# A six-layer cross network on one core: the first half's remainder columns as one load behind the second group, put in order by VectorE, and a first layer without its add

## The chip, the cores and the metric

The kernel runs on one core of one Trainium2 chip. The metric is the device time in microseconds (us) of one execution, as the median of several. The kernel before took 130.63 us (three runs, 130.57 to 130.87). One further execution was recorded by the profiler; it took 130.73 us, and its profile covers a span of 128.9 us. All durations below come from that execution.

## What is computed

The input x0 has 4096 rows of 416 bf16 numbers. Six weight matrices of 416 x 416 and six bias rows are given. Each layer multiplies x0, element by element, with an affine function of the running x, and adds x:

```python
def reference(x0, ws, bs):
    x = x0
    for l in range(ws.shape[0]):
        x = x0 * (x @ ws[l] + bs[l]) + x
    return x
```

In the first layer x is x0 itself, so there the formula is x0 * (x0 @ w + b + 1).

## The kernel before

**Layout.** The work is done transposed: features lie on partitions, rows of x0 along the free axis. The 416 columns are cut into three blocks of 128 (the main blocks, `m` or `k` = 0, 1, 2) and a remainder of 32. The 4096 rows are cut into two halves (`s` = 0, 1) of four groups (`g` = 0 to 3) of 512 rows. `XM[i]` holds the main blocks of x (`XM[0]` those of x0, for good). `XR[i]` holds the remainder: its four bands of 32 partitions are the four groups of a half. `XRd` is a copy of `XR[0]` with its upper and lower 64 partitions exchanged.

**How x0 comes in.** Each group of 512 rows comes by one transposing DMA (`load_x0t`, L75), eight in all, issued on SyncE's queue (SP) in the order (0,0), (0,1), (0,2), (0,3), (1,0) to (1,3). They are called transposed loads here. The 32 remainder columns come as plain row segments of 64 bytes and are transposed by TensorE:

- first half: four loads of 32 KB on ScalarE's queue (`load_xrem0`, L80), each straight into the column order that the transposes want (`xrig[:, 0]`);
- second half: one load of 128 KB on SP's queue (`load_xrem1`, L84) between the transposed loads (1,0) and (1,1), into `xrem`; GpSimd then puts it into column order (L132).

`x0_rem` (L155 to L158) makes four 128x128 transposes into PSUM, and VectorE copies the result three times: to `XR[0]` and, in two halves, to `XRd`. The remainder rows of the first layer's weights (`load_wr0`, L87) come on SP's queue between the transposed loads (0,1) and (0,2), and are spread to the other three bands by ScalarE (L108) and GpSimd (L110). A DMA takes one of eight semaphores in turn, and a DMA whose semaphore was used before waits, on its queue, for that earlier DMA to land.

**The first layer** (`first_layer`, once for each half). TensorE's order in the first half is: the three main blocks of group 0 (`full`, L212, nine matmuls), the four transposes of `x0_rem`, the three main blocks of group 1 (nine matmuls), eight small matmuls with the remainder (`row`, L219), then block 0 of group 2 and of group 3, block 1 of both, block 2 of both, four more `row` matmuls, the remainder's own output (`mm_rem`, L191 and L196), and the second half's four transposes. The second half goes the same way, but takes block by block both groups. ScalarE takes every result out of PSUM with the bias added (`ew_main` L163, `ew_rem` L171), VectorE multiplies by x0 (L164, L172) and adds x (L167, L173).

**After that** come layers 1 to 4, which keep the data in place and are fed by the same three steps (TensorE L179 and L185, ScalarE L163, VectorE L164 and L167), and a last layer that computes untransposed output rows (L325 to L334, ScalarE L352, VectorE L353 and L342) and sends them out.

PSUM has four slots of two banks. Within an engine, instructions run in the order in which they stand; a scheduler may move them unless `tc.keep_in_program_order` pins them.

Of the kernel before, what the change touches and what calls it, by code (L numbers as in the profile page):

```python
# [10 lines left out]
ALU = mybir.AluOpType  # L11
BF16 = mybir.dt.bfloat16
# [4 lines left out]
def kernel(  # L17
# [7 lines left out]
    nc = tc.nc  # L25
    B, D = x0.shape
    L = ws.shape[0]
    P = 128
    NK = 3
    R = D - NK * P  # L30
    assert R == 32 and B == 4096 and D == 416 and L >= 2
    NS = 2
    NG = 4
    CW = 512
# [5 lines left out]
    big = ctx.enter_context(tc.tile_pool(name="big", bufs=1))  # L40
# [4 lines left out]
    x0_v = x0.rearrange("(bt p) d -> p bt d", p=P)  # L45
    out_v = out.rearrange("(bt p) d -> p bt d", p=P)

    ident = const.tile([P, P], BF16)
# [3 lines left out]
    WR = const.tile([P, L, D], BF16)  # L52
# [3 lines left out]
    bM = const.tile([P, NK, L], FP32)  # L56
    bR = const.tile([P, L], FP32)
    X0rows = big.tile([P, NBT, D], BF16)
    XLrows = big.tile([P, NBT, D], BF16)
    scrR = [big.tile([P, 4, P], BF16, name=f"scrR{s}") for s in range(NS)]  # L60
    xrem = big.tile([P, 16, R], BF16)
    xrig = big.tile([P, NS, 4, P], BF16)
    XRd = big.tile([P, NS * CW], BF16)
    XM = [big.tile([P, NK, B], BF16, name=f"XM{i}") for i in range(3)]
    XR = [big.tile([P, NS * CW], BF16, name=f"XR{i}") for i in range(3)]

    def col0(s, g):
        return SW * s + CW * g

    def load_wm(eng, l):  # L70
        eng.dma_start(WM[:, l], ws[l, 0:NK * P, :].rearrange("(k p) n -> p k n", p=P))

    def load_x0t(s, g):
        c0 = col0(s, g)
        nc.sync.dma_start_transpose(out=XM[0][:, :, c0:c0 + CW], in_=x0[c0:c0 + CW, 0:NK * P])  # L75

    def load_xrem0():
        with nc.allow_non_contiguous_dma(reason="64B row segments"):
            for i in range(4):
                nc.scalar.dma_start(xrig[:, 0, i, :].rearrange("p (g r) -> p g r", g=NG), x0_v[:, i:16:4, NK * P:D])  # L80

    def load_xrem1():
        with nc.allow_non_contiguous_dma(reason="64B row segments"):
            nc.sync.dma_start(xrem[:], x0_v[:, 16:32, NK * P:D])  # L84

    def load_wr0():
        nc.sync.dma_start(WR[0:R, 0, :], ws[0, NK * P:D, :])  # L87

    def load_wr(eng, g, l0, l1):
        eng.dma_start(WR[32 * g:32 * g + 32, l0:l1, :], ws[l0:l1, NK * P:D, :].rearrange("l r n -> r l n"))  # L90
# [7 lines left out]
    load_x0t(0, 0)  # L98
    load_wm(nc.scalar, 0)
    nc.scalar.dma_start(bsb[:], bs[:, :])  # L100
    load_x0t(0, 1)
    load_xrem0()
    load_wr0()
    nc.scalar.activation(dz[:, 1:2], dz[:, 0:1], ACT.Identity, bias=dz[:, 0:1], scale=1.0)  # L104
    for g in range(1, NG):
        dst, src = WR[32 * g:32 * g + 32, 0, :], WR[0:R, 0, :]
# [4 lines left out]
    for g in range(2, NG):  # L111
        load_x0t(0, g)
    load_x0t(1, 0)
    load_xrem1()
    for g in range(1, NG):
        load_x0t(1, g)
    load_wm(nc.sync, 1)
# [9 lines left out]
    def fill_wd(l0, l1):  # L127
        for g in range(NG):
            nc.gpsimd.tensor_copy(WD[32 * g:32 * g + 32, l0:l1, g, :], WR[32 * g:32 * g + 32, l0:l1, NK * P:D])  # L129

    fill_wd(0, 1)
    nc.gpsimd.tensor_copy(xrig[:, 1].rearrange("p i (g r) -> p i g r", g=NG), xrem[:].rearrange("p (g i) r -> p i g r", g=NG))  # L132
    fill_wd(1, L)

    wps = psum.tile([P, CW], FP32, tag="ps", name="wps")
# [8 lines left out]
    def bias_setup():  # L144
        pb = psum.tile([P, 4, 8], BF16, tag="ps", name="pb")
        for m in range(NK):
            nc.tensor.transpose(pb[:, m, 0:L], bsb[0:L, 128 * m:128 * m + 128], ident[0:L, 0:L])
        for g in range(NG):
            nc.tensor.transpose(pb[32 * g:32 * g + 32, 3, 0:L], bsb[0:L, NK * P:D], ident[0:L, 0:L], tile_position=(0, 32 * g))
        nc.vector.tensor_copy(bM[:], pb[:, 0:NK, 0:L])  # L150
        nc.vector.tensor_copy(bR[:], pb[:, 3, 0:L])

    def x0_rem(s, tpr):
        for i in range(4):
            nc.tensor.transpose(tpr[:, 128 * i:128 * i + 128], xrig[:, s, i, :], ident[:])  # L155
        for dst, src in ((slice(0, P), slice(0, P)), (slice(64, P), slice(0, 64)), (slice(0, 64), slice(64, P))):
            to = XR[0] if dst == src else XRd
            nc.vector.tensor_copy(to[dst, CW * s:CW * s + CW], tpr[src])  # L158

    def ew_main(l, s, m, h, pt, cur, nxt, pin=False):  # L160
        c0 = col0(s, 2 * h)
        t = tpool.tile([P, 2 * CW], BF16, name="t")
        nc.scalar.activation(t[:], pt[:].rearrange("p a b -> p (a b)"), ACT.Identity, bias=bM[:, m, l:l + 1], scale=1.0)  # L163
        prod = nc.vector.tensor_tensor(out=t[:], in0=t[:], in1=XM[0][:, m, c0:c0 + 2 * CW], op=ALU.mult)  # L164
        if pin:
            tc.keep_in_program_order(prod)
        nc.vector.tensor_tensor(out=nxt[:, m, c0:c0 + 2 * CW], in0=t[:], in1=cur[:, m, c0:c0 + 2 * CW], op=ALU.add)  # L167

    def ew_rem(l, s, pr, curR, nxtR):
        tr = tpool.tile([P, 2 * CW], BF16, name="t")  # L170
        nc.scalar.activation(tr[:, 0:CW], pr, ACT.Identity, bias=bR[:, l:l + 1], scale=1.0)  # L171
        nc.vector.tensor_tensor(out=tr[:, 0:CW], in0=tr[:, 0:CW], in1=XR[0][:, CW * s:CW * s + CW], op=ALU.mult)  # L172
        nc.vector.tensor_tensor(out=nxtR[:, CW * s:CW * s + CW], in0=tr[:, 0:CW], in1=curR[:, CW * s:CW * s + CW], op=ALU.add)  # L173

    def mm_full(l, s, m, g, pts, cur, first, last):
        c0 = col0(s, g)
# [12 lines left out]
    def mm_rem(l, s, pr, cur, curR):  # L189
        for g in range(NG):  # L190
            nc.tensor.matmul(pr[32 * g:32 * g + 32, :], lhsT=WD[:, l, g, :], rhs=curR[:, CW * s:CW * s + CW],  # L191
                             start=True, stop=False, tile_position=(0, 32 * g))
        for k in range(NK):
            for g in range(NG):
                c0 = col0(s, g)
                nc.tensor.matmul(pr[32 * g:32 * g + 32, :], lhsT=WM[:, l, k, NK * P:D], rhs=cur[:, k, c0:c0 + CW],  # L196
                      start=False, stop=(k == NK - 1), tile_position=(0, 32 * g))
# [8 lines left out]
    def first_layer(s):  # L206
        cur, curR, nxt, nxtR = XM[0], XR[0], XM[1], XR[1]

        def full(pt, m, h, gl, after_row):
            c0 = col0(s, 2 * h + gl)  # L210
            for k in range(NK):
                nc.tensor.matmul(pt[:, gl, :], lhsT=WM[:, 0, k, 128 * m:128 * m + 128], rhs=cur[:, k, c0:c0 + CW],  # L212
                                 start=(k == 0 and not after_row), stop=(k == NK - 1 and after_row))

        def row(pt, m, h, opens):
            for gl in range(2):
                rg = 32 * ((2 * h + gl) ^ (2 if m == 1 else 0))
                src = XRd if m == 1 else curR
                nc.tensor.matmul(pt[:, gl, :], lhsT=WR[rg:rg + 32, 0, 128 * m:128 * m + 128],  # L219
                                 rhs=src[rg:rg + 32, CW * s:CW * s + CW],  # L220
                                 start=opens, stop=not opens, tile_position=(rg, 0))

        def ph(m):
            return psum.tile([P, 2, CW], FP32, tag="ps", name=f"ph{m}")

        pa = [ph(m) for m in range(NK)]
        if s == 0:
            for m in range(NK):
                full(pa[m], m, 0, 0, False)
            tp0 = psum.tile([P, CW], BF16, tag="ps", name="tpr")  # L230
            x0_rem(0, tp0[:])
            for m in range(NK):
                full(pa[m], m, 0, 1, False)
        else:
            for m in range(NK):
                for gl in range(2):
                    full(pa[m], m, 0, gl, False)
        pb = [ph(0)]
        row(pa[0], 0, 0, False)
        row(pb[0], 0, 1, True)  # L240
        row(pa[2], 2, 0, False)
        row(pa[1], 1, 0, False)
        for m in range(NK):
            ew_main(0, s, m, 0, pa[m], cur, nxt)
        for m in range(NK):
            if m:
                pb.append(ph(m))
            for gl in range(2):
                full(pb[m], m, 1, gl, m == 0)
        row(pb[1], 1, 1, False)  # L250
        row(pb[2], 2, 1, False)
        pr = psum.tile([P, 2, CW], FP32, tag="ps", name="pr")
        mm_rem(0, s, pr[:, 0, :], cur, curR)
        if s == 0:
            x0_rem(1, pr[:, 1, :].bitcast(BF16)[:, 0:CW])
        for m in range(NK):
            ew_main(0, s, m, 1, pb[m], cur, nxt, pin=(s == 0))
        ew_rem(0, s, pr[:, 0, :], curR, nxtR)

    bias_setup()  # L260
    pe_filler(1, CW)
    for s in range(NS):
        first_layer(s)
# [15 lines left out]
    cur, curR = XM[1], XR[1]  # L279
    for l in range(1, LL):  # L280
        nxt, nxtR = XM[1 + (l % 2)], XR[1 + (l % 2)]
# [29 lines left out]
        cur, curR = nxt, nxtR  # L311

    l = LL
# [97 lines left out]
```

## Time and profile before

| what | value |
|---|---|
| median of three runs | 130.63 us |
| the profiled execution, its time / its span | 130.73 / 128.9 us |
| TensorE (PE) busy | 122.8 us, 95% of the span |
| VectorE (DVE) busy | 106.7 us, 83% |
| ScalarE (ACT) busy | 86.9 us, 67% |
| GpSimd (POOL) busy | 6.3 us, 5% |
| granted TensorE clock, mean | 0.99 |
| share of the chain that ended last | PE 80%, DMA 8%, DVE 5% |
| DVE t<-t,XM L164 and XM<-t,XM L167, 128x1024 | 60 of each, 690 and 697 ns |
| DVE L172 and L173, 128x512 | 10 of each, 419 and 424 ns |
| DVE copies in `x0_rem` L158 | 425 ns (XR), 422 ns (each half of XRd) |
| POOL copy into column order L132 | 665 ns |

The chain that ended last is followed back from the last instruction: at each step to what released it, or to the instruction before it on its engine. Busy shares are averages over stages, so what an edit is worth has to be read in its own stage. A DMA row names the queue that issues it: SPq for SyncE's, ACTq for ScalarE's; its duration is that of the issue, not of the transfer, whose end is called its landing.

### The profile page before, as it was taken

How to read it: one execution, taken by the hardware profiler on the slowest of the kernel's cores; microseconds unless marked ns; L12 is line 12 of the kernel's file. 1: busy time of each engine (PE TensorE's matmuls, PEld its weight loads, DVE VectorE, ACT ScalarE, POOL GpSimd, SP SyncE). 2: the span in 40 equal slices, each digit the busy share in tenths (PEclk: the TensorE clock that was granted, in tenths of full speed). 3: DMA queues.
4: the chain of work that ended last, by engine and by line, in shares of the span. 5: the costliest groups of instructions: out<-in, count | busy, mean ns of one | idle time of the engine just before them, and what ended most of it. 6: DMA issues, size and time to landing. Idle time of an engine off the chain costs nothing.

```text
span 128.9 us, 3971 instructions
## 1 busy us (share of the span) xinstructions
PE 122.8 (95%) x1689; PEld 55.0 (43%) x1691; DVE 106.7 (83%) x195; ACT 86.9 (67%) x99; POOL 6.3 (5%) x18
## 2 busy tenths in 40 slices
PE   7899999999999999999999999999999999999960
PEld 3333343344444454444344444444444345445430
DVE  0032979999999898989898989898989899898991
ACT  0426783987849577848667848668848896569670
POOL 4022200620000000000000000000000000000000
PEclk9999999999999999999999999999999999999996
DMA  3999999999990000000000000000297999995754
GB/s 93 248 200 218 166 164 241 235 330 333 335 324 16 5 0 8 0 0 5 0 5 0 5 0 5 0 5 0 40 167 164 123 226 176 195 311 186 230 179 141
DMA packets 42102, 16.37 MB, mean 127 GB/s; under 512 B 30906, under 2 KB 42084, under 8 KB 42084
## 3 DMA queue, kind: packets, MB, share of 16 engines
q1 hardware_dynamic: 39416, 15.56, 54.4%
q10 hardware_dynamic: 2668, 0.56, 2.4%
q8 instruction: 13, 0.21, 0.7%
q14 instruction: 5, 0.04, 0.1%
HBM read 6.15 MB, written 3.41 MB: 74 GB/s over the span
## 4 chain that ended last, share of the span: by engine, by line
PE 80%; DMA 8%; DVE 5%; issue 2%; SPq 1%; ACT 1%; DVEq 0%
PE pt L179 49%; PE ph L212 9%; DMA XM<-in_x_dram 8%; PE py L325 8%; PE pt L185 5%; PE pr L196 5%; DVE t L353 3%; DVE o L342 2%; PE pr L191 2%; SPq L75 1%; PE py L331 1%; PE ph L219 1%; PE py L334 1%; ACT t L352 1%; PE pr L155 0%
## 5 line engine op out<-in xcount | busy, mean ns | idle before, releaser
L179 PE MATMUL pt<-XM,WM 128*32 128x512 bf16 x1152 | 65.2, 379 | 0.0
L163 ACT ACTIVATE t<-pt,bM 128x1024 bf16<-128x1024 f32 x48 | 49.6, 1115 | 18.3 <-PE pt L185 18.3
L164 DVE TENSOR_TENSOR t<-t,XM 128x1024 bf16<-128x1024 bf16 x60 | 41.4, 690 | 5.3 <-ACT t L163 5.3
L167 DVE TENSOR_TENSOR XM<-t,XM 128x1024 bf16<-128x1024 bf16 x60 | 41.8, 697 | 3.4
L179 PEld LDWEIGHTS <-WM 128*32 128x32 bf16 x1152 | 29.7, 97 | 33.8 <-issue 5.1
L352 ACT CAST t<-py 128x416 bf16<-128x416 f32 (+1 forms) x23 | 14.8, 642 | 4.8 <-PE py L325 2.1
L325 PE MATMUL py<-WM,XM 128*128 128x416 bf16 x96 | 17.7, 340 | 0.0
L212 PE MATMUL ph<-XM,WM 128*128 128x512 bf16 x70 | 16.4, 379 | 0.8 <-DMA XM<-in_x_dram 0.7
L163 ACT ACTIVATE t<-ph,bM 128x1024 bf16<-128x1024 f32 x12 | 12.5, 1113 | 4.4 <-PE ph L219 4.4
L325 PEld LDWEIGHTS <-XM 128*128 128x128 bf16 x96 | 9.0, 98 | 8.5 <-issue 1.4
L353 DVE TENSOR_TENSOR t<-t,X0rows 128x416 bf16<-128x416 bf16 (+1 forms) x23 | 10.4, 455 | 1.2 <-ACT t L352 1.2
L212 PEld LDWEIGHTS <-WM 128*128 128x128 bf16 x72 | 6.8, 97 | 9.1 <-issue 1.8
L342 DVE TENSOR_TENSOR o<-t,XLrows 128x416 bf16<-128x416 bf16 (+1 forms) x23 | 10.3, 453 | 0.0
L171 ACT ACTIVATE t<-pr,bR 128x512 bf16<-128x512 f32 x10 | 6.4, 685 | 2.7 <-PE pr L196 2.1
L196 PE MATMUL pr<-XM,WM 128*32 128x512 bf16 x120 | 8.2, 379 | 0.0
L185 PE MATMUL pt<-XR,WR 32*128 32x512 bf16 x96 | 7.3, 379 | 0.0
L139 PE MATMUL wps<-const-bfloat16-1.0 128*128 128x512 bf16 (+1 forms) x12 | 4.1, 523 | 0.8 <-PEq L395 0.8
L173 DVE TENSOR_TENSOR XR<-t,XR 128x512 bf16<-128x512 bf16 x10 | 4.2, 424 | 0.7
L196 PEld LDWEIGHTS <-WM 128*32 128x32 bf16 x120 | 3.2, 97 | 3.0
L104 ACT ACT_TABLE_LOAD x1 | 1.3, 1283 | 4.4 <-DMA WM<-in_ws_dram 4.4
L172 DVE TENSOR_TENSOR t<-t,XR 128x512 bf16<-128x512 bf16 x10 | 4.2, 419 | 0.0
L129 POOL COPY WD<-WR 32x32 bf16<-32x32 bf16 (+1 forms) x8 | 3.6, 453 | 8.1 <-DMA WR<-in_ws_dram 7.7
(38 smaller groups left out, 30.0 us busy)
## 6 DMA issues: line engine op xcount, KB each, us to landing
X0rows<-in_x_dram SPq DMA_DIRECT2D x4, 832.0 KB, 11.0
out_dram<-o SPq DMA_DIRECT2D x9, 208.0 KB, 2.4
WM<-in_ws_dram SPq DMA_DIRECT2D x5, 312.0 KB
out_dram<-o SPq DMA_DIRECT2D x13, 104.0 KB, 1.7
WR<-in_ws_dram SPq DMA_DIRECT2D x4, 130.0 KB, 4.2
WM<-in_ws_dram ACTq DMA_DIRECT2D x1, 312.0 KB
XM<-in_x_dram SPq DMA_TRANSPOSE x8, 4.9
xrig<-in_x_dram ACTq DMA_DIRECT2D x4, 32.0 KB, 4.1
```

The source lines that it names most:

```text
L163: nc.scalar.activation(t[:], pt[:].rearrange("p a b -> p (a b)"), ACT.Identity, bias=bM[:, m, l:l + 1], scale=1.0)
L164: prod = nc.vector.tensor_tensor(out=t[:], in0=t[:], in1=XM[0][:, m, c0:c0 + 2 * CW], op=ALU.mult)
L167: nc.vector.tensor_tensor(out=nxt[:, m, c0:c0 + 2 * CW], in0=t[:], in1=cur[:, m, c0:c0 + 2 * CW], op=ALU.add)
L171: nc.scalar.activation(tr[:, 0:CW], pr, ACT.Identity, bias=bR[:, l:l + 1], scale=1.0)
L179: nc.tensor.matmul(pts[g // 2][32 * q:32 * q + 32, g % 2, :], lhsT=WM[:, l, k, 128 * m + 32 * q:128 * m + 32 * q + 32], rhs=cur[:, k, c0:c ...
L185: nc.tensor.matmul(pts[g // 2][:, g % 2, :], lhsT=WR[32 * g:32 * g + 32, l, 128 * m:128 * m + 128], rhs=curR[32 * g:32 * g + 32, CW * s:CW ...
L196: nc.tensor.matmul(pr[32 * g:32 * g + 32, :], lhsT=WM[:, l, k, NK * P:D], rhs=cur[:, k, c0:c0 + CW], start=False, stop=(k == NK - 1), tile ...
L212: nc.tensor.matmul(pt[:, gl, :], lhsT=WM[:, 0, k, 128 * m:128 * m + 128], rhs=cur[:, k, c0:c0 + CW], start=(k == 0 and not after_row), sto ...
L325: nc.tensor.matmul(py[:, 0:D], lhsT=cur[:, k, q_cols(q, g)], rhs=WM[:, l, k, :], start=((not closes) and k == 0), stop=(closes and k == NK ...
L342: tc.keep_in_program_order(nc.vector.tensor_tensor(out=o, in0=t, in1=xl, op=ALU.add))
L352: nc.scalar.copy(tv, src)
L353: tc.keep_in_program_order(nc.vector.tensor_tensor(out=tv, in0=tv, in1=X0rows[:, b, :], op=ALU.mult))
```

## The change

1. The first half's remainder is no longer four loads on ScalarE's queue. It is one load of 128 KB on SP's queue, issued between the transposed loads (0,1) and (0,2). It lands in a buffer in row order.
2. VectorE puts it into column order (`by_column`). For the second half GpSimd does this, as before.
3. The load of the first layer's remainder weights moves from SP's queue to ScalarE's, behind the bias load.
4. In the first half TensorE's four transposes move behind blocks 0 and 1 of group 1, ahead of its block 2. In the second half the blocks of the first of two groups go ahead of those of the second.
5. The two exchanged copies `XRd` are made from `XR[0]` in SBUF instead of from PSUM.
6. The first layer's biases get 1 added once (two small VectorE instructions), and its VectorE work is one multiplication instead of a multiplication and an addition.
7. The first layer's VectorE instructions and the transposes are pinned in program order.

TensorE has the same instructions as before, in another order. VectorE loses 12 additions of 128x1024 and 2 of 128x512 and gains one copy and the two small bias instructions. With fewer DMAs ahead, the transposed load (0,2) no longer shares a semaphore with the load (0,0), and does not wait for it.

```diff
-    xrem = big.tile([P, 16, R], BF16)
+    xrem = [big.tile([P, 16, R], BF16, name=f"xrem{s}") for s in range(NS)]
...
-    def load_xrem0():
+    def load_xrem(s):
         with nc.allow_non_contiguous_dma(reason="64B row segments"):
-            for i in range(4):
-                nc.scalar.dma_start(xrig[:, 0, i, :].rearrange("p (g r) -> p g r", g=NG), x0_v[:, i:16:4, NK * P:D])
-
-    def load_xrem1():
-        with nc.allow_non_contiguous_dma(reason="64B row segments"):
-            nc.sync.dma_start(xrem[:], x0_v[:, 16:32, NK * P:D])
+            nc.sync.dma_start(xrem[s][:], x0_v[:, 16 * s:16 * s + 16, NK * P:D])
+
+    def by_column(s, copy):
+        pin(copy(xrig[:, s].rearrange("p i (g r) -> p i g r", g=NG), xrem[s][:].rearrange("p (g i) r -> p i g r", g=NG)))
 
     def load_wr0():
-        nc.sync.dma_start(WR[0:R, 0, :], ws[0, NK * P:D, :])
+        nc.scalar.dma_start(WR[0:R, 0, :], ws[0, NK * P:D, :])
...
     nc.scalar.dma_start(bsb[:], bs[:, :])
+    load_wr0()
     load_x0t(0, 1)
-    load_xrem0()
-    load_wr0()
+    load_xrem(0)
...
-    nc.gpsimd.tensor_copy(xrig[:, 1].rearrange("p i (g r) -> p i g r", g=NG), xrem[:].rearrange("p (g i) r -> p i g r", g=NG))
+    by_column(1, nc.gpsimd.tensor_copy)
...
+        pin(nc.vector.tensor_scalar_add(bM[:, :, 0:1], bM[:, :, 0:1], 1.0))
+        pin(nc.vector.tensor_scalar_add(bR[:, 0:1], bR[:, 0:1], 1.0))
...
-        for dst, src in ((slice(0, P), slice(0, P)), (slice(64, P), slice(0, 64)), (slice(0, 64), slice(64, P))):
-            to = XR[0] if dst == src else XRd
-            nc.vector.tensor_copy(to[dst, CW * s:CW * s + CW], tpr[src])
+        cs = slice(CW * s, CW * s + CW)
+        pin(nc.vector.tensor_copy(XR[0][:, cs], tpr))
+        for dst, src in ((slice(64, P), slice(0, 64)), (slice(0, 64), slice(64, P))):
+            pin(nc.vector.tensor_copy(XRd[dst, cs], XR[0][src, cs]))
...
-        prod = nc.vector.tensor_tensor(out=t[:], in0=t[:], in1=XM[0][:, m, c0:c0 + 2 * CW], op=ALU.mult)
-        if pin:
-            tc.keep_in_program_order(prod)
-        nc.vector.tensor_tensor(out=nxt[:, m, c0:c0 + 2 * CW], in0=t[:], in1=cur[:, m, c0:c0 + 2 * CW], op=ALU.add)
+        if l == 0:
+            pin(nc.vector.tensor_tensor(out=y, in0=t[:], in1=x, op=ALU.mult))
+            return
+        nc.vector.tensor_tensor(out=t[:], in0=t[:], in1=x, op=ALU.mult)
+        nc.vector.tensor_tensor(out=y, in0=t[:], in1=cur[:, m, c0:c0 + 2 * CW], op=ALU.add)
...
         pa = [ph(m) for m in range(NK)]
+        for m in range(NK):
+            full(pa[m], m, 0, 0, False)
         if s == 0:
-            for m in range(NK):
-                full(pa[m], m, 0, 0, False)
+            by_column(0, nc.vector.tensor_copy)
+            full(pa[0], 0, 0, 1, False)
+            full(pa[1], 1, 0, 1, False)
             tp0 = psum.tile([P, CW], BF16, tag="ps", name="tpr")
             x0_rem(0, tp0[:])
+            full(pa[2], 2, 0, 1, False)
+        else:
             for m in range(NK):
                 full(pa[m], m, 0, 1, False)
-        else:
-            for m in range(NK):
-                for gl in range(2):
-                    full(pa[m], m, 0, gl, False)
```

## The prediction

> **What bounds the kernel now.** I read the chain that ended last first, then the busy time by stages, then SyncE's (SP) issues one by one, then the DMA packets of the first 16 us.
>
> The chain, from the start to 17.5 us (start, duration, what):
>
> ```profile
> 0.74 4.85 DMA XM<-in_x_dram
> 5.59 0.02 issue
> 5.61 1.42 SPq L75
> 7.03 0.04 issue
> 7.07 5.07 DMA XM<-in_x_dram
> 12.14 0.04 issue
> 12.19 3.40 PE ph L212 x15
> ```
>
> The first 12.14 us belong to transposed loads: (0,0) lands at 5.59, (0,3) at 12.14, and TensorE (PE) takes its fifteen matmuls behind (0,3) at once. By stages (span; length, then busy us and count of PE, PEld, VectorE, ScalarE, GpSimd; clock, DMA share, GB/s):
>
> ```profile
> 12.19:16.90 4.71, 4.71 (x37) 1.88 (x37) 4.26 (x6) 3.94 (x4) 0.67 (x1) 1.00 1.14 176
> ...
> 26.90:46.20 19.30, 19.30 (x352) 8.69 (x344) 18.42 (x32) 14.23 (x16) 0.00 (x0) 1.00 0.69 205
> 46.20:65.40 19.20, 19.20 (x348) 8.59 (x344) 17.29 (x29) 13.62 (x15) 0.00 (x0) 1.00 0.01 2
> ...
> 103.90:115.60 11.70, 11.70 (x94) 5.83 (x98) 10.66 (x20) 8.49 (x11) 0.00 (x0) 1.00 1.11 242
> ```
>
> From 12.19 us on PE is busy the whole of each of these stages at granted clock 1.00. So the end is the landing of (0,3), plus a block of PE work that the change only reorders, plus a tail. What moves 12.14 moves the end one for one; what VectorE (DVE) or ScalarE saves behind a PE without gaps moves nothing.
>
> **Who sets 12.14.** SP's issues (start, duration):
>
> ```profile
> 2.18 2.58 SPq L75 DMA_TRANSPOSE XM<-in_x_dram  x1
> 4.81 0.57 SPq L87 DMA_DIRECT2D WR<-in_ws_dram  x1
> 5.61 1.42 SPq L75 DMA_TRANSPOSE XM<-in_x_dram  x1
> 7.07 2.04 SPq L75 DMA_TRANSPOSE XM<-in_x_dram  x1
> 9.16 1.70 SPq L75 DMA_TRANSPOSE XM<-in_x_dram  x1
> 10.90 0.58 SPq L84 DMA_DIRECT2D xrem<-in_x_dram  x1
> 11.52 2.93 SPq L75 DMA_TRANSPOSE XM<-in_x_dram  x1
> 14.49 1.41 SPq L75 DMA_TRANSPOSE XM<-in_x_dram  x1
> ```
>
> The reader should see the ends: (0,1) 4.76, (0,2) 7.03, (0,3) 9.11, (1,0) 10.86, then `xrem` 11.48, (1,1) 14.45, (1,2) 15.90. A transposed issue takes 1.4 us when nothing holds it and up to 2.93 us when something does. Loads (0,2) and (0,3) landed 3.0 us after their issue's end (10.01, 12.14). The packets tell what holds an issue (queue q1 is SP's, q10 ScalarE's; packets, MB, share), in 5:7, 7:9 and 13:14.2 us:
>
> ```profile
> q1 hardware_dynamic: 1469, 0.38, 89.4%
> q10 hardware_dynamic: 1353, 0.08, 48.7%
> ...
> q1 hardware_dynamic: 1540, 0.40, 105.0%
> q10 hardware_dynamic: 394, 0.02, 13.4%
> ...
> q1 hardware_dynamic: 1816, 0.12, 134.9%
> ```
>
> A transposed load is 512 rows of 768 bytes, 1536 packets of 256 bytes. SP's queue moves about one in 2 us, and did so in 5:7 us although 1353 small packets, mostly of the four remainder loads, went beside it. Those were nearly free. In 13:14.2 us SP's own remainder load was at the head: 1816 packets but 0.12 MB, so hardly a transposed packet moved, and the issue of (1,1) ended only behind it.
>
> **The change part by part.**
>
> *The remainder load on SP's queue (parts 1 and 3).* The new order (0,1), remainder, (0,2) is that of (1,0), `xrem`, (1,1) in the trace, on the same queue and of the same sizes. From the end of issue (1,0) to that of (1,1) it is 14.45 - 10.86 = 3.59 us; from (0,1) to (0,2) it is now 7.03 - 4.76 = 2.27 us. So (0,2) ends its issue near 4.76 + 3.59 = 8.35, 1.32 us late. For (0,3) behind it I have 1.45 us (15.90 - 14.45, the exact counterpart), 1.75 (10.86 - 9.11) and 2.08 (its own step now): issue end 9.80 to 10.43 against 9.11, landing 12.8 to 13.45. That is +0.69 to +1.32 us; I take +1.0, the middle, since the low end comes from one interval. The gains are within it: the semaphore wait of (0,2) (5.39 to 5.61, 0.2 us) goes, but an issue that is held till 8.35 doesn't feel it; the weights' 0.57 us of issue goes, but the remainder's 0.58 takes its place. ScalarE's queue loses four issues (1.91 to 4.36, 2.45 us) and gains one of about 0.6; its next work waits for weights that now land earlier.
>
> *A page against this.* By the Trainium skill, "DMA: Bandwidth & Descriptors", section "Issuing engines are not separate DMA queues", DMAs of all engines run on the same 16 DMA engines and interleave, whoever issued them. Read strictly, a move between queues costs nothing, and the sum would be 0. The intervals 3.59 and 2.27 disagree in this case: order in one queue counted. It is the second case below.
>
> *TensorE's side up to group 3 (parts 2, 4, 5).* (0,1) lands without the small packets near 4.76 + 3.0 = 7.8 (now 8.54). Six matmuls at 0.216 us end at 9.1. The remainder lands at 4.81 + 4.3 (the landing time of `xrem`) = 9.1. DVE's copy into column order isn't in the trace: between 0.42 (DVE's L158 of the same size) and 0.67 (GpSimd's L132, the same copy); I take 0.45, nearer to its own engine's row: 9.6. Four transposes (0.33 in the chain, 0.4 with their tail): 10.0. Block 2 of group 1, 0.65: 10.7. The copy to `XR` 0.43: 10.45. The two `XRd` copies from SBUF: at most 0.42 each (the same from PSUM), at least 0.06 (DVE's shortest row, L93): 10.6 to 11.3. Eight `row` matmuls, 0.54: 11.9 at the latest. Group 2's three matmuls, 0.65: 12.5. This lies in front of 12.8 to 13.45, so it costs nothing; the cover is 0.3 us or more. Without it (if (0,3) landed at 12.14 still) this chain would cost up to 0.3.
>
> *DVE's savings (part 6).* 12 x 0.697 + 2 x 0.424 = 9.2 us less, less 0.45 for the copy and two tiny additions, each between 0.06 (L93) and 0.18 (L150), beside an idle engine before 8.6 us. Covered by PE: it has no gap behind 12.19, and DVE has caught up anyway by 44.4 us, where it waits 0.43 for ScalarE. So 0 on the end.
>
> *Second half's order (part 4).* Block 2 needs a PSUM slot 1.3 us behind the start of the half (17.22) and not 2.6. ScalarE frees it at 16.96 + 1.11 = 18.07, before 18.5. Worth 0; up to 0.2 if a semaphore's delay eats it. Load (1,1) is needed later than now, (1,2) and (1,3) shift with PE.
>
> *Sum.* +1.0 us. The profiled execution took 130.73, of which 128.9 are span; the median is 130.63, 0.1 lower, and I add to that: **131.6 us**, by its own terms 131.3 to 132.0.
>
> **The rivals.** About 0.2% (0.26 us) is what a measurement of this kernel can tell from no change.
>
> 1. *Forecast, slower, 0.73.* The remainder load stands in the way of the transposed loads. The price decides from an issue end of (0,2) behind 7.3 us.
> 2. *No change, 0.15.* The DMA engines carry the same packets up to (0,3), 1536 x 3 + 2048 in all behind 4.76 us, and now do it by 10.9 us either way. Then (0,3) lands at 12.14, and TensorE's own chain adds 0 to 0.3: 130.6 to 130.9. For it: the engines are shared. Against: 13:14.2 us.
> 3. *Faster, 0.12.* The remainder's packets fill the slow first part of (0,2) as those on q10 filled 5:7 us, and (0,1) drains sooner alone. With 1.8 us a load (the step of 9.1 to 10.9 us) (0,1), (0,2) and (0,3) drain by 4.76 + 3 x 1.8 = 10.16, not 10.86: (0,3) would land 0.7 earlier, and its own chain, if all copies are short, lets PE take it 0.5 earlier: 130.1 to 130.3. It decides from an issue end of (0,2) before 7.0 us. Against: (1,1) was held until `xrem` had gone.
>
> **How the numbers follow.** The likeliest case gives 131.6, with its own range 131.2 to 132.1 (0.69 to 1.32 rounded out by the 0.2 of the PSUM slot). Its tails and the whole of case 2 are needed to leave out 2 in 10 or less, so the range goes from 130.5 to 132.1. Faster 0.12, same 0.15, slower 0.73 are the three cases.
>
> **What would show it.** Right: the issue of (0,2) takes about 2.9 us and ends near 8.35; the chain has a landing of XM near 13.1 just ahead of fifteen matmuls of L212; everything from there to the end stands about 1 us later; VectorE has some 9 us less. Wrong: (0,2) ends its issue near 7 us, or the wait ahead of those matmuls is not on a DMA, or PE shows gaps behind it (a slot in the second half at 18 to 19 us).

## The result and the profile after

The changed kernel took 132.13 us (median of six executions, 131.80 to 133.91) against 130.67 us for the kernel before (130.37 to 130.87). The ratio is 1.0098, 95% interval 1.0073 to 1.0123: **1% slower**. The execution of 133.91 us ran at a mean granted clock of 0.978, the others at 0.993 to 0.999; it is left out of the ratio and comes up again in the last section. The profiled execution took 131.80 us with a span of 130.0 us, 1.07 us and 1.1 us more than those of before. It is the fastest of the six, so the trace holds 1.07 of the 1.46 us between the medians; a second profile follows in run 7.

The chain that ended last, changed kernel, up to TensorE's fifteen matmuls (start, duration, what):

```profile
2.17 2.67 SPq L75
...
4.89 0.58 SPq L82
...
5.53 2.43 SPq L75
...
7.99 4.84 DMA XM<-in_x_dram
12.84 0.04 issue
12.88 3.40 PE ph L222 x15
```

The reader should see that SP's queue itself is now on the chain: load (0,1) issued to 4.84, the remainder load L82 to 5.47, then the issue of (0,2), which took 2.43 us instead of 1.42 and ended at 7.95 instead of 7.03. What held it shows in the packets of SP's queue in 6.5:7.7 us (packets, MB, share):

```profile
q1 hardware_dynamic: 1905, 0.12, 108.2%
```

1905 packets with 0.12 MB are the remainder's row segments of 64 bytes; hardly a transposed packet of 256 bytes moved in this time. Load (0,3) lands at 12.84 instead of 12.14, and the fifteen matmuls start at 12.88 instead of 12.19, **0.69 us later**.

By stages, changed kernel (span; length, then busy us and count of PE, PEld, DVE, ACT, POOL; clock, DMA share, GB/s):

```profile
12.19:13.30 1.11, 0.42 (x2) 0.19 (x2) 0.80 (x2) 1.11 (x2) 0.00 (x0) 1.00 1.21 198
13.30:18.00 4.70, 4.70 (x40) 1.98 (x39) 0.91 (x3) 2.90 (x4) 0.61 (x1) 1.00 1.11 158
18.00:22.20 4.20, 4.20 (x26) 1.65 (x24) 3.18 (x7) 1.34 (x2) 0.00 (x0) 1.00 1.31 198
...
28.00:47.30 19.30, 19.30 (x352) 8.69 (x345) 15.71 (x27) 14.24 (x16) 0.00 (x0) 1.00 0.67 199
```

PE stands for 0.69 of the 1.11 us in the first row and is full in the others, the second half's new order (18.00:22.20) included. VectorE has less to do (98.7 us in all, 106.7 before) and nothing follows from it. The last VectorE instruction ends at 127.06 instead of 126.37, again 0.69 later. The shift is made in the first 13 us and carried to the end.

The span grew by 1.06, so 0.37 us are still to be found, and they lie behind the last output. SP's final wait for the output's DMAs (total, times, longest, in us), before and after:

```profile
SPq L406 <- DMA out_dram<-o: 1.5, 4, 0.5
```

```profile
SPq L417 <- DMA out_dram<-o: 1.6, 2, 1.3
```

In both traces SP ends with five waits, each for two semaphores, the eight DMA semaphores among them. Before, the last output's semaphore is in the fifth pair: the outputs came in in the order of the waits, four short ones, and the fifth ended 0.05 us behind the last landing (128.12 to 128.17). After, it is in the second pair: the first wait is one of 1.3 us for a late output, and the pairs behind the last landing are worked off one by one, 0.06 us each: 128.81 to 129.05, 0.24 us. The change issues three DMAs fewer, so the last output takes another of the eight semaphores. The rest, 0.18 us, is a drain of ScalarE, the last engine to report (129.66 to 129.80). That drain stands in the second profile of the changed kernel too (run 7), and in neither of the two kernels of runs 1 and 2, which end in the same order of waits. No run shows why.

### The profile page after: what moved, and what is told of

It is laid out like the page before. It is cut to its first block, busy times and chain, and to the rows that moved or that the text cites. A ratio compares the mean times of both kernels' runs of the same rounds, so it can differ in the third digit from the quotient of the medians.

```text
span 130.0 us, 3959 instructions
## 1 busy us (share of the span) xinstructions
PE 123.3 (95%) x1691; PEld 55.0 (42%) x1691; DVE 98.7 (76%) x184; ACT 86.8 (67%) x99; POOL 5.1 (4%) x18
## 3 DMA queue, kind: packets, MB, share of 16 engines
HBM read 6.15 MB, written 3.41 MB: 74 GB/s over the span
## 4 chain that ended last, share of the span: by engine, by line
PE 80%; DVE 5%; SPq 5%; DMA 4%; issue 2%; ACT 1%; DVEq 0%
PE pt L189 49%; PE ph L222 9%; PE py L336 8%; PE pt L195 5%; PE pr L206 5%; SPq L75 5%; DMA XM<-in_x_dram 4%; DVE t L364 3%; DVE o L353 2%; PE pr L201 2%; PE py L342 1%; PE ph L229 1%; PE py L345 1%; ACT t L363 1%; SPq L82 0%
## 5 line engine op out<-in xcount | busy, mean ns | idle before, releaser
L172 DVE TENSOR_TENSOR t<-t,XM 128x1024 bf16<-128x1024 bf16 x48 | 33.0, 687 | 5.4 <-ACT t L168 5.4
L140 PE MATMUL wps<-const-bfloat16-1.0 128*128 128x512 bf16 (+1 forms) x12 | 4.8, 589 | 0.8 <-PEq L406 0.8
L183 DVE TENSOR_TENSOR XR<-t,XR 128x512 bf16<-128x512 bf16 x8 | 3.4, 426 | 0.7
L201 PE MATMUL pr<-XR,WD 128*32 128x512 bf16 x40 | 3.9, 381 | 0.0
```

The source lines that it names most:

```text
L172: nc.vector.tensor_tensor(out=t[:], in0=t[:], in1=x, op=ALU.mult)
```

## The experiments

**Theory.** On SP's queue a transposed load's issue ends only when what stands ahead of it has gone. A remainder load ahead of group 3 so delays (0,3), whatever else is changed, and TensorE is bound by (0,3). **Rival A:** the packets count, not the queue. **Rival B:** TensorE's order, the detour over VectorE or the first layer's form costs the time. Each kernel ran beside the kernel before on the same chip.

### 1. The remainder on ScalarE's queue

```diff
-            nc.sync.dma_start(xrem[s][:], ...)
+            (nc.scalar if s == 0 else nc.sync).dma_start(xrem[s][:], ...)
```

> The changed kernel, but the first half's one remainder load is issued on ScalarE's queue, behind the first layer's remainder weights. Queue-order theory (the remainder load stands ahead of group 2 on SP's queue): the issue of (0,2) ends near 7.0 us again and (0,3) lands at 11.8 to 12.3 instead of 12.84, so 130.4 to 131.0 us. Rival A (the same packets on shared DMA engines, whichever queue): (0,3) still lands near 12.8, 131.9 to 132.3. Rival B (TensorE's new order and the detour over VectorE set the restart): fifteen matmuls of L222 still start near 12.9 with the wait on something other than a DMA, about 131.9.

Measured: 130.79 us, ratio 1.0006 (0.9995 to 1.0018). Its chain:

```profile
2.17 6.42 DMA XM<-in_x_dram
...
8.63 1.46 PE ph L222 x6
10.09 0.23 PE tpr L158 x4
10.31 0.65 PE ph L222 x3
10.96 0.58 PE ph L229 x8
11.54 0.32 PE ph L222
...
11.91 3.62 PE ph L222 x16
```

The loss is gone with one word. (0,2) ends its issue at 6.60 and (0,3) lands at 11.36, 1.48 us earlier than in the changed kernel with the same packets: Rival A falls. Yet the time is only that of the kernel before, and the chain says why: (0,1), which the remainder's packets now run beside, lands at 8.59 (7.26 in the changed kernel), and from there TensorE has work without a gap. (Its end also has the changed kernel's 0.24 us of waits.) The four transposes (0.23 us in the chain) stand in that work, while in the kernel before they filled the wait for (0,1). The remainder is also issued earlier here (2.26 against 4.89 us), which could be the gain instead of the queue; run 12, where it is issued at 0.74 on SP's queue and (0,3) lands late, speaks against that.

### 2. Only the loads; 3. only the first layer

```diff
-                nc.scalar.dma_start(xrig[:, 0, i, :]...)
+            nc.sync.dma_start(xrem0[:], x0_v[:, 0:16, NK * P:D])
...
-        nc.sync.dma_start(WR[0:R, 0, :], ws[0, NK * P:D, :])
+        nc.scalar.dma_start(WR[0:R, 0, :], ws[0, NK * P:D, :])
...
+            tc.keep_in_program_order(nc.vector.tensor_copy(xrig[:, 0]..., xrem0[:]...))
```

> The kernel before with only the loads changed: first half's remainder as one load on SP's queue behind (0,1), put in order by VectorE, weights' load on ScalarE's queue; the transposes stay behind group 0, XRd comes from PSUM, the first layer keeps multiplication and addition. Queue-order theory: (0,3) lands at 12.6 to 13.1 and the end moves by the same 0.5 to 0.9 plus the little that the changed kernel has at its very end, 131.3 to 132.1 us. Rival B (TensorE's order, the first layer's form and the pins are what costs): 130.5 to 130.9.

```diff
+        nc.vector.tensor_scalar_add(bM[:, :, 0:1], bM[:, :, 0:1], 1.0)
+        nc.vector.tensor_scalar_add(bR[:, 0:1], bR[:, 0:1], 1.0)
...
+        if l == 0:
+            tc.keep_in_program_order(nc.vector.tensor_tensor(out=nxt[...], in0=t[:], in1=XM[0][...], op=ALU.mult))
+            return
```

> The kernel before with only the first layer's form changed: 1 added to its biases, one multiplication for multiplication and addition, pinned; the loads as before. Queue-order theory: VectorE is about 9 us less busy, TensorE restarts at 12.2 as before and has no gap behind, 130.5 to 130.9 us. Rival (VectorE's new order, or the add's absence, is part of the loss or hides a gain): outside 130.4 to 131.0.

Measured: the loads alone, 131.61 us, ratio 1.0069 (1.0049 to 1.0089), (0,3) landing at 12.79, restart at 12.83. The first layer alone, 130.80 us, 1.0008 (0.9993 to 1.0023), restart at 12.16. Rival B falls: the loads carry the loss, and VectorE's additions were free.

### 4. Two remainder loads on SP's queue; 5. the same with PE kept busy

```diff
     load_xrem(0)
+    with nc.allow_non_contiguous_dma(reason="64B row segments"):
+        nc.sync.dma_start(xspare[:], x0_v[:, 16:32, NK * P:D])
```

> The changed kernel with a second load of the same size on SP's queue (128 KB that nothing reads) right behind the remainder load. Queue-order theory: each such load takes about 1.2 us of the queue to itself, so (0,3) lands 1.0 to 1.4 us later than in the changed kernel beside it, near 14.0, and the time rises by as much, 132.8 to 133.4 us. Rival (its packets fill gaps of the transposed loads): less than 0.4 more than the changed kernel.

Measured: (0,3) lands at 14.24, 1.2 to 1.4 us behind the changed kernel's two profiles (12.84 and, beside it, 13.04). The dose fits. The time does not: two executions took 132.56 and 133.15 (ratio 1.0156, 1.0119 to 1.0194), four took 134.6 to 134.9. The profiled one is of the four. Its stages, columns as above:

```profile
10.50:13.90 3.40, 1.27 (x10) 0.47 (x5) 1.75 (x4) 3.10 (x3) 0.00 (x0) 1.00 1.09 201
13.90:17.30 3.40, 3.02 (x8) 1.06 (x8) 0.69 (x1) 1.14 (x2) 0.00 (x0) 0.50 1.03 153
17.30:20.00 2.70, 2.70 (x25) 1.09 (x27) 0.00 (x0) 0.48 (x1) 0.61 (x1) 1.00 1.09 203
```

TensorE was busy 1.27 of 3.40 us, waiting for groups 2 and 3, and then had the clock at 0.50 for one stretch of that length: the fifteen matmuls took 4.88 us instead of 3.40. So a longer wait cost its own length and 1.5 us more. The next kernel fills the wait:

```diff
-        row(pb[0], 0, 1, True)
+        if s:
+            row(pb[0], 0, 1, True)
...
+        if s == 0:
+            for _ in range(10):
+                pin(nc.tensor.matmul(pb[0][:, 0, :], lhsT=warm[:, 0:P], rhs=warm[:, 0:CW], start=True, stop=True))
+            row(pb[0], 0, 1, True)
```

> The kernel with two loads on SP's queue, and ten matmuls of constants (2.2 us, into a bank that is opened anew behind them) in the place where TensorE waited for groups 2 and 3. In the run without them TensorE stood still for 1.04 and 1.42 us there and the granted clock fell to half for 3.4 us, and the fifteen matmuls took 4.88 us instead of 3.40. Theory that the standing still lowers the clock: clock 1.00 throughout, (0,3) still lands near 14.2, fifteen matmuls in 3.4, about 1.5 us less than the run without them, 132.6 to 133.4 us in all executions. Rival (the clock fell by chance or through the load itself): times of 134 and more come again.

Measured: 133.10 us, four executions from 133.03 to 133.15, ratio 1.0191 (1.0176 to 1.0206); (0,3) lands at 13.88, the clock is 1.00 from 5.92 us to 128.80, and groups 2 and 3 run at speed in the chain:

```profile
13.27 0.32 PE ph L232 x2
13.59 3.99 PE ph L225 x18
```

None of the four executions has the 1.5 us that four of six had without the filling, so work without use took them off: the clock followed TensorE's standing still, not the load. The two kernels ran on different chips, and the two executions that kept the clock without it, 132.56 and 133.15 us, took no longer than these.

### 6 to 8. The end of the program

> The changed kernel with three more tiny loads (0.8 KB each, of bias rows that nothing reads) behind the last loads of the start, so that the last output's DMA again takes the last of the eight semaphores in the order of the final waits. The changed kernel's profile has 0.26 us from the last landing (128.76) to the last of SP's waits (129.05 at its end), the kernel before 0.05. Theory that this is a second part of the loss: the waits end within 0.1 us of the last landing and the time is 0.15 to 0.25 below the changed kernel's, 131.7 to 132.0. Rival (the end is a matter of chance): no change in what lies between last landing and end, 132.0 to 132.3.

> The changed kernel once more, for a second profile and a time on the same chip as the three next to it: 131.6 to 132.2 us, (0,3) landing at 12.5 to 12.9, fifteen matmuls behind it without a gap, and 0.2 us or more between the last landing and the last of SP's waits.

> The changed kernel with three more tiny loads, as before, now beside the changed kernel itself on one chip. Theory that the order of the final waits is a second part of the loss: 0.1 to 0.25 us less than the changed kernel in this call, and the waits end within 0.1 us of the last landing. Rival (chance): within 0.1 of it.

The edit is the same in both kernels with more DMAs:

```diff
+    spare = const.tile([4, D], BF16)
...
+    for g in range(3):
+        nc.sync.dma_start(spare[g:g + 1, :], bs[g:g + 1, :])
```

Measured: 131.64 us, ratio 1.0065 (1.0043 to 1.0088), on the chip of runs 1 to 3; on a second chip 131.68, 1.0060 (1.0038 to 1.0081), beside the changed kernel's 131.84, 1.0075 (1.0052 to 1.0098). The traces are clear: the waits end 0.04 us behind the last landing in both kernels with three more loads, and 0.24 behind it in both profiles of the changed kernel. The times point the same way, but 0.16 us between overlapping intervals is not more than a hint.

### 9. The end alone

```diff
+    spare = const.tile([5, D], BF16)
...
+    for g in range(5):
+        nc.sync.dma_start(spare[g:g + 1, :], bs[g:g + 1, :])
```

> The kernel before with five more tiny loads (0.8 KB, of bias rows that nothing reads) at the end of the start's loads, so that the last output's DMA takes the same place among the eight semaphores as in the changed kernel. Theory that the order of the final waits costs by itself: the last of SP's waits ends 0.2 to 0.25 us behind the last landing (0.05 in the kernel before), and the time is 0.1 to 0.3 above it. Rival: the waits end within 0.1 of the last landing, or the time is the same within 0.1.

Measured: 130.93 us against 130.53, ratio 1.0031 (1.0020 to 1.0042), 0.26 to 0.55 us. SP's final wait in this kernel, which is otherwise the kernel before:

```profile
SPq L409 <- DMA out_dram<-o: 1.6, 2, 1.3
```

It is the changed kernel's pattern, 0.24 us from the last landing (127.87) to the end of the waits (128.11). Five tiny loads in the middle of the kernel slow its end: the order of the final waits costs by itself. The time is a little more than the 0.2 us that the trace shows, and where the rest of it lies is open. (Its profiled execution took 130.68 us all the same: (0,3) landed at 11.88 in it, 0.26 us earlier than in the kernel before, with the same loads.)

### 10 to 12. Three tries at a faster kernel

Clear SP's queue up to group 2, with TensorE's order as before:

```diff
     load_x0t(0, 1)
+    load_x0t(0, 2)
     load_xrem0()
...
-        nc.sync.dma_start(WR[0:R, 0, :], ws[0, NK * P:D, :])
+        nc.scalar.dma_start(WR[0:R, 0, :], ws[0, NK * P:D, :])
...
```

> The kernel before with SP's queue cleared up to group 2: the transposed load (0,2) is called ahead of the first half's four remainder loads (so that it takes a semaphore of its own and waits for no landing), and the remainder weights go to ScalarE's queue behind those four. TensorE's order, VectorE's work and the first layer as before. Queue-order theory: (0,2) ends its issue near 6.6 and (0,3) lands at 11.3 to 11.7 as with the load on ScalarE's queue; TensorE, whose transposes stay ahead of the landing of (0,1), comes to group 3 at about 11.75 instead of 12.19, so 130.1 to 130.5 us. Rival (the landing of (0,1) near 8.6, or the weights, bind as well): 130.5 to 130.9.

Measured: 130.62 us against 130.89, ratio 0.9986 (0.9970 to 1.0002); not told apart from no change. (0,3) lands at 11.64 as expected, but TensorE starts group 1 only at 8.76, and has work from there on:

```profile
8.30 0.46 PE tpr L155 x2
8.76 2.09 PE ph L212 x9
```

Two things hold it there within 0.05 us of each other: (0,1) has landed at 8.71, and the last of the four transposes, which waits for the last part of the remainder (landed at 8.48), ends at 8.76. It was the rival: (0,1), with the remainder's packets beside it, binds as well.

The remainder in four parts on ScalarE's queue, two of them held until (0,0) has landed:

```diff
...
-    load_xrem(0)
+    load_x0t(0, 2)
+    load_xrem0(0)
+    load_xrem0(1)
+    load_x0t(0, 3)
...
+    load_xrem0(2)
+    load_xrem0(3)
...
-    for g in range(2, NG):
-        load_x0t(0, g)
```

> The changed kernel with the remainder load in four parts on ScalarE's queue, two issued early and two held until the load (0,0) has landed, and nothing but transposed loads on SP's queue up to group 3. What the runs so far say: SP's queue free of the remainder gives (0,3) near 11.4, but the packets beside (0,1) put its landing from 7.2 to 8.6, and TensorE is then bound by that. If half of the packets go beside (0,2) instead, (0,1) lands near 7.9 and TensorE reaches group 3 near 11.5 to 11.8: 130.1 to 130.5 us. Rival (parts issued that late land behind 9.3 and hold the four transposes): 130.6 to 131.2.

Measured: 131.18 us, ratio 1.0028 (1.0015 to 1.0040). (0,1) lands at 7.77, as meant, and (0,3) at 11.46. But the parts that were issued at 5.39 and 5.80 land at 9.44 and 9.91, and the transposes wait for them:

```profile
5.80 4.11 DMA xrem<-in_x_dram
...
10.34 0.40 PE tpr L165 x4
```

The rival again. The remainder load first of all:

```diff
...
+    load_xrem0()
     load_x0t(0, 0)
...
```

> Remainder load first of all on SP's queue, ahead of (0,0), put in order by VectorE; TensorE's order, the copies and the first layer as in the kernel before; weights' load on ScalarE's queue; three tiny loads more, so that the final waits stand as before. SP then issues (0,0) 0.6 us later, but the remainder's packets run while the DMA engines wait for the first transposed load anyway (before 2.7 us). Theory (only what stands ahead of (0,3) in the queue and the DMA engines' busy time count): (0,0) lands near 6.0 to 6.4, (0,1) at 7.6 to 8.0, (0,3) at 11.4 to 12.0, TensorE goes without a gap from (0,1) or waits little, 130.0 to 130.6 us. Rival (the whole queue shifts by the remainder's 1.2 us): (0,3) near 12.8, 131.3 to 131.8.

Measured: 132.02 us, ratio 1.0123 (1.0084 to 1.0161); four executions took 131.84 to 132.11 and two, at a granted clock of 0.98, 133.04 and 133.16.

```profile
7.97 5.24 DMA XM<-in_x_dram
13.21 0.04 issue
13.25 3.40 PE ph L215 x15
```

My expectation that it would use idle time was wrong. (0,0) lands at 7.29 instead of 5.59, (0,1) at 9.05, and (0,3) at 13.21, a little later than with the load behind (0,1). Wherever it was tried ahead of group 3, a remainder load on SP's queue delayed (0,3): by 0.7 and 0.9 us behind (0,1), by another 1.2 to 1.4 for a second load there, by 1.1 ahead of (0,0). No version beat both kernels beyond its interval.

## Why the prediction was right, and where not

**Mechanism.** As forecast: (0,2)'s issue is held by the remainder load, a landing of XM stands ahead of fifteen matmuls, everything behind is shifted by one amount, and VectorE's savings change nothing. The chance of 0.73 for it came from one comparison inside the trace, (1,0) - `xrem` - (1,1), whose counterpart the change made.

**Size of the landing.** The step was +1.0 (0.69 to 1.32) for (0,3); measured +0.70 in the first profile, +0.90 in the second. The term that was mis-sized is the interval from the end of issue (0,1) to that of (0,2): 3.59 forecast, 3.11 measured (4.84 to 7.95). The counterpart's issue took 2.93 us, this one 2.43; in the changed kernel's own trace the issue of (1,1) took 2.58. A single interval had been taken as exact: in run 9, whose first loads are those of the kernel before, the counterpart itself took 3.08 (10.88 to 13.96). The next step, 1.77 (7.95 to 9.72), lay among the three rows. So the issue of (0,3) ended at 9.72, below the 9.80 to 10.43 of the forecast, and the landing, 3.12 us behind it instead of 3.03, came just inside the range. One landing is not exact either: (0,3) landed between 11.88 and 12.14 in the three traces with the loads of the kernel before (the kernel before, runs 3 and 9), and between 12.56 and 13.04 in the five with those of the changed kernel (the result, runs 2, 6, 7 and 8).

**A term that was missing.** The count of DMAs was worked out for the wait of (0,2) on its semaphore, and not carried to the end of the program, where the same rotation costs 0.2 us in the trace and 0.26 to 0.55 in time (run 9). ScalarE's late drain, 0.18 us, was not in the sum either. Together they filled what the landing fell short of: +1.0 in the forecast; 0.69 + 0.19 + 0.18 = 1.06 us of span in the first profile, 0.90 + 0.19 + 0.19 = 1.28 in the second. The medians rose by 1.46 (132.13 against 130.67) and by 0.95 (131.84 against 130.89); the first stands at the upper end of the range, 130.5 to 132.1. That the sum came near is in part chance.

**TensorE's side up to group 3.** It was to be ready by 12.5 at the latest; in the trace group 2's matmuls start at 11.09, held by their load for 0.25, and PE stands from 11.90 (0.98 us in all). Hidden, as said, with more cover. (0,1) had landed at 7.26, earlier than the 7.8 of the forecast: the four remainder loads of the kernel before were called nearly free, and so they were for the issue of (0,2), but (0,1) landed at 8.54 beside them. The copy into column order took 0.29 us on VectorE, below both ends that I gave (0.42 and 0.67), and the two `XRd` copies 0.61 together. VectorE lost 8.0 us of work, not some 9.

**The second half's order and the first layer** cost and gave nothing, as said (18.00:22.20 full; ratio 1.0008 for the first layer alone).

**The rivals.** "No change" had the DMA engines' shared work behind it, and the page "DMA: Bandwidth & Descriptors" of the Trainium skill (section "Issuing engines are not separate DMA queues"). The runs differ from that reading: the same packets gave (0,3) at 11.36 from ScalarE's queue and at 12.84 from SP's. What the faster case needed, an earlier landing of (0,3), came true in runs 1 and 10 (0.8 and 0.5 us earlier), and gave almost nothing, because (0,1) then binds, with the remainder's packets beside it. The case had put the remainder behind (0,1), and no run with it there had (0,3) early, so its price of 0.5 us was not tested. In the kernel before there was little to win by (0,3) alone, as TensorE's wait for it shows (in brackets):

```profile
12.19 0.59 PE L212 MATMUL ph<-XM,WM 128*128 128x512 bf16 x2 [0.20 <-DMA XM<-in_x_dram]
```

**The range** had no term for the clock; an execution of 133.91 us lies far outside it.

## What to carry to other kernels

Read a queue as a line: what a load costs there is the time that the loads behind it wait, and a trace with the same order of loads elsewhere gives that time better than packet counts do, if several such intervals are taken and not one. Ask of each gain what lands next: in the kernel before, TensorE had work from the landing of (0,1) up to 0.2 us before that of (0,3), and every place tried for the remainder load delayed one of the two, or came too late for the transposes. After a change in the number of DMAs, look at the last microsecond too.

## What the runs showed of the hardware

**The clock falls without a long standstill.** In the kernel with two loads on SP's queue TensorE stood 1.04 and 1.42 us, with matmuls between, and 1.27 busy of 3.40 us were few enough to get half the clock for the next 3.4 us. By the Trainium skill, "TensorE: Matmul & The Clock Gate", section "What's actually happening", the gate looks at windows of 3413 ns that run freely and goes cold after an idle one. The length agrees; that the window must be idle doesn't. In this trace the full clock begins at 3.66 us, the half clock at 13.90 and the full clock again at 17.31, three such lengths and one; the stretch of 3.41 us ahead of 13.90 had TensorE busy for 1.28. In the changed kernel's second profile the full clock begins at 3.60, and the third stretch from there, 10.43 to 13.84, was busy for 2.03 us and was not followed by a lower clock. If the work in such a stretch decides, its limit lies between 1.28 and 2.03 us by these two traces. Windows that run freely would explain why two of six executions of that kernel escaped. The changed kernel stood for 0.98 us in its first profile and kept its clock; its one execution of 133.91 us at clock 0.978, and the two of run 12 above 133 us, may have been caught in the same way, but there is no trace of them.

**A load on ScalarE's queue landed only near SP's transposed load.** In the changed kernel the 26 KB of weights were issued on ScalarE's queue at 1.91 and landed at 5.91, just behind (0,0) at 5.65; in run 10 they were issued at 6.02 and landed at 9.71, near (0,2) at 9.92; in run 12 they were issued at 2.20 and landed at 7.07, near (0,0), which was late there (7.29). That the transposed load holds them up, though it stands in the other queue, is a reading of these three traces; no run tested it.
